# Contracting 64 rows in half the array: the third part of the first layer in the seven smallest experts

## The chip, the cores and the metric

The kernel runs on one core of one Trainium2 chip. The metric is device microseconds of one execution, the median of three. Engines are named as the profile names them: PE is TensorE's matmuls, PEld its weight loads, DVE is VectorE, ACT is ScalarE, POOL is GpSimd, SP is SyncE.

## The reference

A gated recurrent attention over 4 batches, 8 heads, 768 steps and head size 40 gives 3072 tokens of 320 features; a two-level mixture of 16 experts follows. Each token picks a group and, in it, an expert, and only that expert's two layers are applied to it:

```python
for g in range(G):                       # 4 groups
    mask_g = g_idx == g                  # g_idx = argmax(x @ w_group)
    xg = x[mask_g]
    e_logits = xg @ w_expert[g]
    e_idx = np.argmax(e_logits, axis=1)
    ...
    for e in range(Eg):                  # 4 experts of a group
        mask_e = e_idx == e
        h = np.maximum(xg[mask_e] @ w1[g, e], 0.0)      # 320 -> 1024
        ye = h @ w2[g, e]                               # 1024 -> 320
        out[tok_idx] = combined[:, None] * ye
```

## The kernel before

The attention comes first, in units of 128 steps of one batch. Its rows `x` go to DRAM as 384 columns, the 320 features and then the last 64 of them a second time (`store`). Tokens are routed while the attention runs. Then the experts follow one after another, ordered by how many tokens they have, the largest first. Expert `r` has room for `CAPS[r]` tokens; the last seven, `FULL` (`r` = 9 to 15), have room for 160, 144, 144, 144, 128, 128 and 96. This number is `W` (`W1` in `expert`).

For each expert its token rows are gathered (`load_x`), turned on PE (`turn_tasks`, L314) into `xhl`, features on partitions and tokens along the free dimension, and two layers are computed. The 320 features are three parts of the contraction, `k` = 0, 1, 2, of 128, 128 and 64 rows. The first-layer weights are laid out by the host as three blocks of 128 rows; the third holds rows 256 to 319 twice, in partitions 0 to 63 and again in 64 to 127.

In a `FULL` expert both layers' operands are kept so that float32 products come out exactly enough: the first layer multiplies plain float32 tiles, and each such matmul is two instructions on PE (48 in the profile for 24 in the code). The first layer's 1024 outputs are 8 groups of 128 (`NF`), two of them side by side in one PSUM bank `psh`, from the pool `ps_h` with three buffers. Each group is opened by its `k` = 0 product. The third product contracts all 128 partitions, with the lower half of `xhl[:, 2]` set to zero by POOL (L691); ACT copies the rest of `xhl` in two pieces per block of tokens (L692, L693).

`relu` empties a bank. Where `W` is 160 or 144 it is three steps: DVE writes the last 32 or 16 tokens to `hf` (L720), ACT writes the rounded part of `hh` (L722), and DVE the remainder of `hh` (L725). Where `W` is 128 or 96, `hf` falls away. After each bank one quarter of the next expert's second-layer weights is split into two parts, by ACT (L651) and DVE (L653); this is `between`. After the first layer PE turns the next expert's tokens (L314) and then runs the second layer (L796 to L798 for a block of tokens over 64, three products for each of the 8 groups; L788 for the 16 or 32 tokens that are left over, in four column strips). Its sums `po` are scaled into `y` (L808, or L810 to L813 for the left-over tokens, on ACT and DVE) and scattered to the output by POOL (L592).

```python
W1, rest = W, key[0] > 1 and mo == 32          # rest: the last 32 or 16 tokens apart
...
if rest:
    nc.vector.tensor_scalar(hf[:, f:f + per, :], src[:, :, W:], 0.0, None, op0=ALU.max)
act = nc.scalar.activation(hr, src, AF.Relu)
```

The code up to unit 22 of the attention is issued in the order written; after that the framework's scheduler orders each engine's queue from its own estimate of when operands are ready, with the order of the code as priority. Each engine works its queue in order. The bank named `av` belongs to the pool `ps_1` and serves the attention and the third token block of wide experts.

Of the kernel before, what the change touches and what calls it, by code (L numbers as in the profile page):

```python
# [7 lines left out]
F32 = mybir.dt.float32  # L8
F32R = mybir.dt.float32r
BF16 = mybir.dt.bfloat16  # L10
# [8 lines left out]
P = 128  # L19
# [6 lines left out]
F = 1024  # L26
NF = F // P
# [26 lines left out]
def bc(ap, shape):  # L54
    return ap.broadcast_to(list(shape))
# [3 lines left out]
def lstm_moe(ctx: ExitStack, tc: tile.TileContext, gates, qkT, nat, og, wcat, w1, w2, cst, out):  # L59
    nc = tc.nc  # L60
    enter = ctx.enter_context
    mm = nc.tensor.matmul
# [8 lines left out]
    const = enter(tc.tile_pool(name="const", bufs=1))  # L71
# [6 lines left out]
    ones_b = const.tile([P, P], BF16, name="ones_b")  # L78
# [10 lines left out]
    ohsum = [const.tile([P, NE], BF16, name=f"ohsum{i}") for i in range(2)]  # L89
    sep = const.tile([1, 1], F32, name="sep")  # L90
    neg_b = const.tile([P, P], BF16, name="neg_b")
    wk2 = enter(tc.tile_pool(name="wk2", bufs=2))
    ps_1 = enter(tc.tile_pool(name="ps_1", bufs=1, space=PSUM))
    post = enter(tc.tile_pool(name="post", bufs=2, reuse_waits="tile"))
# [545 lines left out]
    pools = {}  # L640
# [36 lines left out]
    def turn_tasks(key, W, xg, banks=None):  # L677
        t = {}

        def one(i, m):  # L680
            if i == 0:
                pool = pools["xhl"][len(xhls) % len(pools["xhl"])]
                sh, dt = ([P, 3, W], F32) if key[0] in FULL else ([P, 3, 2, W], F32R)
                t["x"] = xhls[key] = pool.tile(sh, dt, name="xhl", bufs=1)
            xhl, g = t["x"], xg[i]
            pool, tag = (banks or ((ps_1, "tp"), (ps_1, "lg"), (ps_1, "av")))[i]
            tp = pool.tile([P, 3, P], F32, name="tpm", tag=tag)
            turned(tp, g)
            if key[0] in FULL:
                if i == 0:  # L690
                    nc.gpsimd.memset(xhl[64:P, 2, :], 0.0)  # L691
                nc.scalar.copy(xhl[:, 0:2, i * P:i * P + m], tp[:, 0:2, 0:m])  # L692
                nc.scalar.copy(xhl[0:64, 2, i * P:i * P + m], tp[0:64, 2, 0:m])  # L693
                return
            xh = xhl[:, :, 0, i * P:i * P + m]
            nc.scalar.copy(xh, tp[:, :, 0:m])  # L696
            nc.vector.tensor_tensor(xhl[:, :, 1, i * P:i * P + m], tp[:, :, 0:m], xh.bitcast(F32), op=ALU.subtract)

        return [lambda i=i, m=m: one(i, m) for i, m in enumerate(blocks(W))]

    def expert(key, W, ws, xg, idx, between=(), then=None, last=None):
        xhl = xhls[key]
# [14 lines left out]
        def relu(f, per, src):  # L717
            hr = hh[:, f:f + per, 0:W]
            if rest:
                nc.vector.tensor_scalar(hf[:, f:f + per, :], src[:, :, W:], 0.0, None, op0=ALU.max)  # L720
                src = src[:, :, 0:W]
            act = nc.scalar.activation(hr, src, AF.Relu)  # L722
            for dst, t in ((slice(wl, wl + nf), slice(0, nf)), (slice(nf + mo, wl), slice(nf, W))):
                if t.start < t.stop:
                    nc.vector.scalar_tensor_tensor(hh[:, f:f + per, dst], src[:, :, t], 0.0, hr.bitcast(F32)[:, :, t],  # L725
                                                   op0=ALU.max, op1=ALU.subtract)
            return act

        if key[0] in FULL:
            w1s = w1st[key[0]]  # L730
            for f in range(0, NF, 2):
                ps = pools["ps_h"].tile([P, 512], F32, name="psh")
                for g in range(2):
                    for k in range(3):
                        s = slice(k * F + (f + g) * P, k * F + (f + g + 1) * P)
                        ins = mm(ps[:, g * W1:(g + 1) * W1], w1s[:, s], xhl[:, k, :], start=(k == 0), stop=(k == 2))  # L736
                relu(f, 2, ps[:, 0:2 * W1].rearrange("p (q w) -> p q w", q=2))
                do(between, 1)
        elif key in NARROW:
            xw, xh = [xhl[:, k].rearrange("p a w -> p (a w)") for k in range(3)], [xhl[:, k, 0, :] for k in range(2)]  # L740
            for f in range(0, NF, 2):
                hs = pools["hp"].tile([P, 2, W], F32, name="hs", bufs=2)
                for g in range(2):
                    ps = pools["ps_h"].tile([P, 512], F32, name="psh")
                    s0 = slice((f + g) * P, (f + g + 1) * P)
                    s1 = slice(F + (f + g) * P, F + (f + g + 1) * P)
                    mm(ps[:, 0:2 * W], w1h[:, s0], xw[0], start=True, stop=False)
                    mm(ps[:, 0:W], w1l[:, s0], xh[0], start=False, stop=False)
                    mm(ps[:, 0:W], w1l[:, s1], xh[1], start=False, stop=False)
                    mm(ps[:, 0:2 * W], w1h[:, s1], xw[1], start=False, stop=False)  # L750
                    ins = mm(ps[:, 0:2 * W], wsk[:, s0], xw[2], start=False, stop=True)
                    nc.scalar.copy(hs[:, g, :], ps[:, W:2 * W])
                    nc.vector.tensor_tensor(hs[:, g, :], hs[:, g, :], ps[:, 0:W], op=ALU.add)
                act = relu(f, 2, hs)
                if key[0] == 0:
                    do(between, 1)
        else:
            per = 2 if W1 <= 256 else 1
            for f in range(0, NF, per):
                ps = pools["ps_h"].tile([P, 512], F32, name="psh")  # L760
                for g in range(per):
                    s0 = slice((f + g) * P, (f + g + 1) * P)
                    s1 = slice(F + (f + g) * P, F + (f + g + 1) * P)
                    xh, xl = [xhl[:, k, 0, :] for k in range(3)], [xhl[:, k, 1, :] for k in range(3)]
                    todo = [(w1h, s0, xh[0]), (w1h, s0, xl[0]), (w1h, s1, xh[1]), (w1h, s1, xl[1]), (wsk, s0, xh[2]),
                            (wsk, s0, xl[2]), (w1l, s0, xh[0]), (w1l, s1, xh[1])]
                    for n, (w, s, x) in enumerate(todo):
                        ins = mm(ps[:, g * W1:(g + 1) * W1], w[:, s], x, start=(n == 0), stop=(n == len(todo) - 1))  # L768
                relu(f, per, ps[:, 0:per * W1].rearrange("p (q w) -> p q w", q=per))
                if per == 2 or f % 2:  # L770
                    do(between, 1)
# [206 lines left out]
    with tc.manual_schedule():  # L978
        nc.sync.dma_start(G[:, 0], gates[0:BH])
        nc.scalar.dma_start(cs, cst)  # L980
        nc.scalar.dma_start(G[:, 1], gates[BH:2 * BH])
        nc.scalar.dma_start(G4, gates[2 * BH:])
        nc.vector.memset(ones_b, 1.0)
        nc.vector.memset(sep, 0.0)
        nc.scalar.activation(sep, sep, AF.Exp)
        busy(11)
        nc.vector.memset(ones4, 1.0)
        nc.vector.memset(Dl[:, 0, 0:1], 0.0)
        nc.vector.memset(Apc[96:P], 0.0)
        for t in qkp[0:2]:  # L990
            nc.gpsimd.memset(t[0:Z], 0.0)
        load_qk(0)
        loads(0)
        load_o(0)
        load_qk(1)
        loads(1)
        loads(2)
        nc.scalar.copy(sel_b, cs[:, C_SEL:C_SEL + B * H])
        nc.scalar.copy(lt_b, cs[:, C_LT:C_LT + P])
        nc.scalar.activation(neg_b, ident, AF.Copy, scale=NEG)  # L1000
        sums.append(gate_sums(0))
        sum_on(9)
        for t in kws:
            nc.gpsimd.memset(t, 0.0)
        for t in qkp[2:]:
            nc.gpsimd.memset(t[0:Z], 0.0)
        nc.gpsimd.memset(Cflat, 0.0)
        nc.gpsimd.tensor_copy(id_b, ident)
        decay(0, 0)
        decay(0, 1, pool=ps_1, tag="lg")  # L1010
        scores(0)
        keyw(0)
        masked(0, 0)
        masked(0, 1)
        carried(0)
        carried2(0)
        sums.append(gate_sums(1))
        decay(1, 0)
        values(0)
        gate_o(0)  # L1020
        decay(1, 1, pool=ps_1, tag="lg")
        state(0)
        sum_on(3)
        keyw(1)
        nc.gpsimd.iota(tokid, pattern=[[P, NBLK]], base=0, channel_multiplier=1)
        nc.gpsimd.tensor_copy(keyb, cs[:, C_15E:C_15E + NE])
        nc.gpsimd.tensor_copy(base_b, cs[:, C_BASE:C_BASE + NE])
        nc.gpsimd.memset(ohsum[0], 0.0)
        loads(3)
        nc.sync.dma_start(wc, wcat)  # L1030
        unit(1, first=True)
        sum_on(9)
        sums.append(later_sums())
        sum_on(1)
        for u in range(2, 10):
            unit(u)
            do(due if u in (2, 6) else [])
            sum_on({2: 2, 3: 3, 4: 2, 5: 9}.get(u, 0))
# [211 lines left out]
```

## Time and profile before

| | |
|---|---|
| median of three runs | 399.18 us |
| the three runs | 398.45, 399.18, 400.91 us |
| the profiled execution | 398.51 us, of which the span from first to last instruction is 396.9 us |
| mean granted clock of TensorE in it | 0.981 |
| busy in the span | PE 379.4 us (96%), DVE 267.0 (67%), ACT 212.8 (54%), POOL 175.0 (44%) |

The span leaves 1.6 us of the execution's time outside. Busy time of PE is modelled for pipelined matmuls: several are in flight at a time, so the pace of a group is read from starts, and not from the mean duration of one instruction. A row of the timeline gives start, time from the first start to the last end, engine, line, what is written from what, and the count; in brackets is the idle time before it.

### The profile page before, as it was taken

What the parts mean: (1) busy time and instruction counts of PE and PEld (TensorE: products, weight loads), DVE (VectorE), ACT (ScalarE), POOL (GpSimd) and SP (SyncE); (2) the same over time, 40 slices, a digit from 0 to 9 for tenths busy, and PEclk for the clock granted to TensorE, in tenths of its full rate; (3) what the DMA queues carried; (4) which work ended last, traced back from release to release, by engine and by line L of the source; (5) the groups of instructions that cost most, each with busy time, mean ns of one, the idle gap of its engine ahead of it and who ended that gap; (6) DMA issues with size and microseconds to landing.
All of it is one profiled execution on the core that took longest, in us unless ns stands there. A gap on an engine that the chain in (4) does not pass through costs nothing.

```text
span 396.9 us, 9817 instructions
## 1 busy us (share of the span) xinstructions
PE 379.4 (96%) x3673; PEld 349.4 (88%) x3673; DVE 267.0 (67%) x702; ACT 212.8 (54%) x544; POOL 175.0 (44%) x231
## 2 busy tenths in 40 slices
PE   8989999999999977999999999999999999999994
PEld 4778998889899866799999998999999998888994
DVE  4777777998888944874957768756745666555520
ACT  5765565666656501625655566656655645445520
POOL 7445576476675544356432206352142315232310
PEclk9999999999999988699999999999999999999999
DMA  7976559999898217029951369996664537887700
GB/s 235 274 225 207 156 80 308 269 322 228 190 304 152 88 23 215 3 61 335 411 207 53 112 250 362 414 310 232 248 226 151 185 110 253 318 307 269 282 18 10
DMA packets 28340, 83.38 MB, mean 210 GB/s; under 512 B 11463, under 2 KB 15550, under 8 KB 24708
## 3 DMA queue, kind: packets, MB, share of 16 engines
q1 hardware_dynamic: 22724, 64.74, 52.1%
q0 software_dynamic: 5232, 17.65, 13.2%
q8 instruction: 29, 0.48, 0.5%
q10 hardware_dynamic: 336, 0.36, 0.3%
q14 instruction: 19, 0.16, 0.2%
HBM read 72.97 MB, written 9.99 MB: 209 GB/s over the span
## 4 chain that ended last, share of the span: by engine, by line
PE 71%; issue 8%; DVE 8%; DMA 7%; POOL 2%; ACT 1%; POOLq 1%; DVEq 0%; SPq 0%; ACTq 0%
PE psh L768 11%; PE av L284 10%; PE psh L736 6%; PE po L796 5%; PE po L798 5%; PE po L797 5%; PE sp L212 5%; PE it L237 4%; DMA itab<-tokid,slot 3%; PE aw L185 3%; PE it L256 2%; PE tpm L314 2%; PE po L788 2%; DMA w1s<-in_w_dram 2%; PE busy L127 2%
## 5 line engine op out<-in xcount | busy, mean ns | idle before, releaser
L195 ACT ACTIVATE ab<-aw,bcol 128x128 f32<-128x128 f32 x192 | 54.6, 371 | 38.0 <-PE aw L185 36.1
L592 POOL DMA_INDIRECT out_dram<-y,ix x32 | 36.1, 1128 | 70.3 <-ACT y L808 61.8
L588 POOL DMA_INDIRECT xg<-x_d,ix x32 | 35.8, 1119 | 64.7 <-DMA ix<-itab 40.0
L796 PE MATMUL po<-w2h,hh 128*128 128x320 f32 (+3 forms) x200 | 63.1, 316 | 0.8 <-ACT hh L722 0.8
L798 PE MATMUL po<-w2h,hh 128*128 128x320 f32 (+3 forms) x200 | 61.9, 310 | 0.0
L797 PE MATMUL po<-w2l,hh 128*128 128x320 f32 (+3 forms) x200 | 61.7, 309 | 0.0
L768 PE MATMUL psh<-xhl,w1hl 128*128 128x256 f32 (+5 forms) x336 | 53.9, 290 | 0.9 <-ACT xhl L696 0.4
L653 DVE TENSOR_TENSOR w2l<-w2s,w2h 128x640 fp32r<-128x640 f32 x52 | 41.0, 818 | 17.2 <-ACT w2h L651 17.1
L284 PE MATMUL av<-nt,pt 128*128 128x128 f32 x384 | 49.1, 283 | 2.3 <-DVE pt L217 2.3
L284 PEld LDWEIGHTS av<-nt,pt 128*128 128x128 f32 x384 | 46.3, 197 | 3.2 <-DVE pt L217 3.2
L768 PEld LDWEIGHTS psh<-xhl,w1hl 128*128 128x128 f32 x336 | 46.7, 193 | 1.9 <-PE psh L768 0.8
L722 ACT ACTIVATE hh<-psh 128x256 fp32r<-128x256 f32 (+5 forms) x68 | 29.1, 431 | 35.3 <-DVE hf L720 17.6
L736 PEld LDWEIGHTS psh<-xhl,w1s 128*128 128x128 f32 x336 | 40.9, 191 | 2.9 <-ACT y L808 2.1
L736 PE MATMUL psh<-xhl,w1s 128*128 128x144 f32 (+3 forms) x336 | 42.5, 285 | 0.2
L725 DVE SCALAR_TENSOR_TENSOR hh<-psh,hh 128x256 fp32r<-128x256 f32 (+4 forms) x76 | 32.7, 445 | 14.7 <-ACT hh L722 13.7
L217 DVE TENSOR_TENSOR pt<-sp,ab 128x512 f32<-128x512 f32 x48 | 30.9, 686 | 14.6 <-PE sp L212 11.3
L808 ACT ACTIVATE y<-po,xg 128x320 f32<-128x320 f32 (+3 forms) x25 | 13.2, 529 | 49.5 <-PE po L798 48.6
L796 PEld LDWEIGHTS po<-w2h,hh 128*128 128x128 f32 (+3 forms) x200 | 36.5, 182 | 2.2 <-ACT hh L722 1.1
L798 PEld LDWEIGHTS po<-w2h,hh 128*128 128x128 f32 (+3 forms) x200 | 36.4, 182 | 0.2
L797 PEld LDWEIGHTS po<-w2l,hh 128*128 128x128 f32 (+3 forms) x200 | 36.4, 182 | 0.0
L651 ACT CAST w2h<-w2s 128x640 fp32r<-128x640 f32 x52 | 35.1, 725 | 0.9 <-DMA w2s<-in_w_dram 0.9
L496 POOL DMA_INDIRECT itab<-tokid,slot x24 | 27.1, 1129 | 16.6 <-DVE slot L430 6.6
(217 smaller groups left out, 733.0 us busy)
## 6 DMA issues: line engine op xcount, KB each, us to landing
w1s<-in_w_dram SPq DMA_DIRECT2D x12, 1536.0 KB, 8.1
w2s<-in_w_dram SPq DMA_DIRECT2D x9, 1280.0 KB, 9.4
nt<-in_nat_dram SPq DMA_DIRECT2D x24, 324.0 KB, 6.4
qk<-in_qkT_dram SPq DMA_DIRECT2D x24, 320.0 KB, 7.5
x_d<-x SPq DMA_DIRECT2D x24, 192.0 KB, 5.9
sig<-in_og_dram SPq DMA_DIRECT2D x6, 640.0 KB, 8.2
w1hl<-in_w_dram SPq DMA_DIRECT2D x3, 1280.0 KB, 10.1
w1s<-in_w_dram SPq DMA_DIRECT2D x4, 768.0 KB, 7.2
```

The source lines that it names most:

```text
L195: rt["exp"] = nc.scalar.activation(st_[u]["ab"][:, r, j, :], aw[:, j, :], AF.Exp, bias=bcol[:, c, i:i + 1])
L284: ins = mm(av[:, i:i + P], t["pm"][r][:, pr, :], nt[:, o:o + P], start=True, stop=True)
L588: return nc.gpsimd.indirect_dma_start(out=o, out_offset=None, in_=src, in_offset=bass.IndirectOffsetOnAxis(ap=idx, axis=0))
L592: return nc.gpsimd.indirect_dma_start(out=out, out_offset=bass.IndirectOffsetOnAxis(ap=idx, axis=0), in_=y, in_offset=None, bounds_check=N ...
L651: nc.scalar.copy(a, src[:, s])
L653: lows.append(lambda: nc.vector.tensor_tensor(o[rows], src[rows, s], a[rows].bitcast(F32), op=ALU.subtract))
L725: nc.vector.scalar_tensor_tensor(hh[:, f:f + per, dst], src[:, :, t], 0.0, hr.bitcast(F32)[:, :, t], op0=ALU.max, op1=ALU.subtract)
L736: ins = mm(ps[:, g * W1:(g + 1) * W1], w1s[:, s], xhl[:, k, :], start=(k == 0), stop=(k == 2))
L768: ins = mm(ps[:, g * W1:(g + 1) * W1], w[:, s], x, start=(n == 0), stop=(n == len(todo) - 1))
L796: mm(po[0:m], hh[:, f, t], w2h[:, s], start=st0, stop=False)
L797: mm(po[0:m], hh[:, f, t], w2l[:, s], start=False, stop=False)
L798: ins = mm(po[0:m], hh[:, f, tl], w2h[:, s], start=False, stop=sp0)
```

## The change

For the seven `FULL` experts the first layer's order changes. All four PSUM banks of the layer are taken at once, three `psh` and the bank `av`. Each is opened by one bfloat16 matmul of zeros (weights `zero_b`, 64 rows) over its whole width of `2 * W1` columns. Then come all eight third parts, each as a contraction of 64 rows: the banks 0 and 2 use partitions 0 to 63 of weights and tokens, the banks 1 and 3 use partitions 64 to 127, in turn. Then come the first and second parts of all eight groups, bank after bank, each bank followed by its `relu` and one task of `between`. The lower half of `xhl[:, 2]` holds the second copy of the 64 features and is no longer zeroed, and one ACT copy per block takes all three parts. `zero_b` is a new constant of 128x128 bfloat16, set by POOL near the start.

```diff
+    zero_b = const.tile([P, P], BF16, name="zero_b")
...
             if key[0] in FULL:
-                if i == 0:
-                    nc.gpsimd.memset(xhl[64:P, 2, :], 0.0)
-                nc.scalar.copy(xhl[:, 0:2, i * P:i * P + m], tp[:, 0:2, 0:m])
-                nc.scalar.copy(xhl[0:64, 2, i * P:i * P + m], tp[0:64, 2, 0:m])
+                nc.scalar.copy(xhl[:, :, i * P:i * P + m], tp[:, :, 0:m])
                 return
...
         if key[0] in FULL:
             w1s = w1st[key[0]]
-            for f in range(0, NF, 2):
-                ps = pools["ps_h"].tile([P, 512], F32, name="psh")
+            banks = [pools["ps_h"].tile([P, 512], F32, name="psh") for _ in range(3)]
+            banks.append(ps_1.tile([P, 512], F32, name="psh", tag="av"))
+
+            def part(i, g, k, rs, **kw):
+                s = k * F + (2 * i + g) * P
+                return mm(banks[i][:, g * W1:(g + 1) * W1], w1s[rs, s:s + P], xhl[rs, k, :], **kw)
+
+            halves = slice(0, 64), slice(64, P)
+            for i in range(4):
+                rs = halves[i % 2]
+                mm(banks[i][:, 0:2 * W1], zero_b[rs], bc(ones_b[rs, 0:W1 // 2].unsqueeze(1), (64, 4, W1 // 2)),
+                   start=True, stop=False)
+            for i in (0, 2):
                 for g in range(2):
-                    for k in range(3):
-                        s = slice(k * F + (f + g) * P, k * F + (f + g + 1) * P)
-                        ins = mm(ps[:, g * W1:(g + 1) * W1], w1s[:, s], xhl[:, k, :], start=(k == 0), stop=(k == 2))
-                relu(f, 2, ps[:, 0:2 * W1].rearrange("p (q w) -> p q w", q=2))
+                    for r in range(2):
+                        part(i + r, g, 2, halves[r], start=False, stop=False)
+            for i in range(4):
+                for g in range(2):
+                    for k in range(2):
+                        ins = part(i, g, k, slice(0, P), start=False, stop=(g == 1 and k == 1))
+                relu(2 * i, 2, banks[i][:, 0:2 * W1].rearrange("p (q w) -> p q w", q=2))
                 do(between, 1)
...
         for t in kws:
             nc.gpsimd.memset(t, 0.0)
+        nc.gpsimd.memset(zero_b, 0.0)
         for t in qkp[2:]:
             nc.gpsimd.memset(t[0:Z], 0.0)
```

## Rows read from the trace of the kernel before

**Rows 1.** Page, part 1: busy us, share of the span, instructions.

```profile
PE 379.4 (96%) x3673; PEld 349.4 (88%) x3673; DVE 267.0 (67%) x702; ACT 212.8 (54%) x544; POOL 175.0 (44%) x231
```

**Rows 2.** Busy time by stretch: PE, PEld, DVE, ACT, POOL, then PEclk, DMA share, GB/s.

```profile
340.90:347.70 6.80, 6.73 (x57) 6.54 (x55) 6.26 (x15) 3.48 (x8) 2.51 (x2) 1.00 0.78 322
347.70:352.60 4.90, 4.90 (x43) 3.88 (x41) 0.59 (x2) 1.90 (x8) 1.37 (x3) 1.00 0.93 330
```

**Rows 3.** Timeline of PE: the first layer of experts 9, 11, 13, 15, and its end.

```profile
317.10 6.68 PE L736 MATMUL psh<-xhl,w1s 128*128 128x160 f32 x48
323.62 0.82 PE L314 MATMUL tpm<-cs,xg 128*128 128x128 f32 x6
...
340.85 6.46 PE L736 MATMUL psh<-xhl,w1s 128*128 128x144 f32 x48
347.14 0.82 PE L314 MATMUL tpm<-cs,xg 128*128 128x128 f32 x6
...
364.04 5.62 PE L736 MATMUL psh<-xhl,w1s 128*128 128x128 f32 x48
369.50 0.49 PE L314 MATMUL tpm<-cs,xg 128*128 128x128 f32 x3
...
382.55 5.50 PE L736 MATMUL psh<-xhl,w1s 128*128 128x96 f32 x48
387.83 0.37 PE L796 MATMUL po<-w2h,hh 128*96 128x320 f32 x1
```

**Rows 4.** Timeline of PE, narrow windows in expert 10's first layer.

```profile
329.10 0.39 PE L736 MATMUL psh<-xhl,w1s 128*128 128x144 f32 x1
...
329.10 0.64 PE L736 MATMUL psh<-xhl,w1s 128*128 128x144 f32 x3
...
329.10 4.68 PE L736 MATMUL psh<-xhl,w1s 128*128 128x144 f32 x36
...
333.83 0.61 PE L736 MATMUL psh<-xhl,w1s 128*128 128x144 f32 x3
```

**Rows 5.** Timeline of PE, narrow windows around the attention's scores and carried products.

```profile
101.74 0.22 PE L185 MATMUL aw<-Apc,sel_b 128*128 128x128 bf16 x1
...
101.89 0.49 PE L212 MATMUL sp<-qk 64*128 64x128 f32 x4
...
101.89 1.16 PE L212 MATMUL sp<-qk 64*128 64x128 f32 x16
...
103.74 0.28 PE L237 MATMUL it<-Cflat,qk 64*128 64x128 f32 x2
103.95 0.23 PE L185 MATMUL aw<-Apc,sel_b 128*128 128x128 bf16 x1
```

**Rows 6.** Timeline of PE near the start: bfloat16 products of 512 columns.

```profile
6.29 0.38 PE L182 MATMUL aw<-neg_b,lt_b 128*128 128x512 bf16 x1
6.50 0.38 PE L185 MATMUL aw<-Apc,sel_b 128*128 128x128 bf16 x4
```

**Rows 7.** Groups of DVE from 280 us on: count, busy us, mean ns, idle before.

```profile
L653 DVE TENSOR_TENSOR w2l<-w2s,w2h 128x640 fp32r<-128x640 f32 x20 | 15.6, 817 | 8.5 <-ACT w2h L651 8.4
L725 DVE SCALAR_TENSOR_TENSOR hh<-psh,hh 128x256 fp32r<-128x256 f32 x24 | 10.0, 418 | 2.0 <-ACT hh L722 1.5
L812 DVE TENSOR_TENSOR y<-y,po 16x320 f32<-16x320 f32 x9 | 4.4, 483 | 0.3
L720 DVE TENSOR_SCALAR hf<-psh 128x32 f32<-128x32 f32 x12 | 2.2, 180 | 1.1 <-PE psh L736 1.1
```

**Rows 8.** Waits from 314 us on: us in total, times, longest us.

```profile
ACT hh L722 <- DVE hf L720: 12.8, 15, 2.2
```

**Rows 9.** Timeline of POOL, and of PE, near the start.

```profile
9.60 0.28 POOL L1008 CAST id_b<-cs 128x128 bf16<-128x128 f32 x1
9.85 0.93 POOL L224 TENSOR_TENSOR kw<-nt,ab 128x320 f32<-128x320 f32 x1
...
11.69 0.67 PE L256 MATMUL it<-nt,kw 128*64 128x41 f32 x16
```

## The prediction, made before the run

> **What bounds the kernel now.** I read the page's busy shares first: PE is at 96% and no other engine is over 67% [rows 1]. The share alone doesn't say that the changed stretch is bound by PE, so the second view is the busy time by stretch, for the first and the second layer of one of the seven experts [rows 2]: PE is busy 6.73 of 6.80 us and 4.90 of 4.90 us, at full granted clock (1.00, the 2.4 GHz level). DVE is the one to watch beside it: 6.26 us of the first layer's stretch, but only 0.59 of the second's. In the third view, the timeline of PE, one expert's first layer starts right behind the other's second layer, and the turning products behind that [rows 3]. So what is taken from PE in this stretch comes off the end of the kernel, unless a wait takes its place. The DMA share is 0.78 and 0.93 in the two stretches [rows 2]; the period is 11.75 us (329.10 to 340.85 [rows 4, 3]) and would be about 8% shorter, so the mean share would go from 0.84 to about 0.91. The weights of an expert are asked for almost two periods ahead, so I count no wait for them.
>
> **The pace of the first layer.** All 48 instructions of an expert go through PE in turn. At `W` = 160 it is 6.52 us / 48 = 136 ns each (317.10 to 323.62 [rows 3]). At 144, from the third to the 36th, (4.68 - 0.64) / 33 = 122 ns [rows 4]. At 128, (5.46 - 0.10) / 48 = 112 ns, with 0.10 us for a slow first instruction, explained below. At 96, 5.28 / 48 = 110 ns [rows 3]: hardly less than at 128, so there something other than the token columns sets the pace. A third of these 48, 16 per expert, is the third part.
>
> **What halves cost.** The trace has float32 products in halves: the attention's scores, 16 instructions in turn on partitions 0 to 63 and 64 to 103, 128 columns each. From the fourth to the sixteenth they take (1.16 - 0.49) / 6 = 112 ns for two [rows 5], against 112 ns for one over all rows at the same width. So two halves run in the time of one, weight loads included. The 16 become 8 pairs at the pace above, and 8 paces are saved: 1.09 us at 160, 0.98 at 144 (three experts), 0.89 at 128 (two), 0.88 at 96. Together 6.70 us.
>
> The Trainium skill, "TensorE: Matmul & The Clock Gate", section "LDWEIGHTS (loading the stationary operand)", speaks against this: a load's time goes by its columns, so 32 rows cost what 128 cost. If the loads of two halves came one after the other, the 6.70 us would be nothing. The scores' row contradicts that for halves in turn (two loads of 128 columns within 112 ns), and the same page, section "Part 3: Packing small matmuls — row/col tiling", says that a load overlaps with matmuls in other rows. It stays as a rival with a small chance.
>
> **A wait that goes.** In experts 10, 11 and 12 PE stands still before the fourth bank: the 36th instruction ends at 333.78, the third of the fourth bank at 334.44, 0.66 us later, where three paces are 0.37 [rows 4]. That is 0.29 us. `ps_h` has three buffers, and the fourth bank waits for the first to be emptied, which DVE does late: ACT's `hh` waits 12.8 us in all for DVE's `hf` [rows 8]. With four banks at once this wait has no place any more: 3 x 0.29 = 0.87 us saved. The other experts show no such gap: 5.46 us at 128 and 6.52 at 160 are 48 even paces.
>
> **The zeros.** Four matmuls of `2 * W1` columns in bfloat16. A product of 512 such columns takes 0.21 us over all rows (6.29 to 6.50 [rows 6]), 0.41 ns a column, with a moving operand that repeats as the zeros' does. No row has bfloat16 in halves. At best two run together, as in the scores: two pairs are 0.26, 0.24, 0.21 and 0.16 us at the four widths, 1.55 us in all seven. At worst they run one by one, 3.10 us. I take 1.55, since the scores are the nearest row and differ only in type; the 1.55 between stays in the range.
>
> **Changes between whole rows and halves.** Entering halves, the scores start 0.15 us after the last `aw` (101.74 to 101.89 [rows 5]), where `aw` products follow each other at (0.38 - 0.22) / 3 = 0.05 us [rows 6]: 0.10 more. Leaving, `aw` starts 0.21 us after the last pair (103.74 to 103.95), 0.10 over a pair's 0.11. The first float32 product after such a change takes 0.39 us (329.10 [rows 4]); two more add only 0.25, so an ordinary one is about 0.29: another 0.10. Leaving thus costs 0.20, seven times: 1.40. Experts 9, 14 and 15 come from whole rows and pay 0.10 on entering: 0.30. Experts 10 to 13 come from the column strips of L788 and pay a change already, 0.10 of it for a slow first float32, which zeros in bfloat16 may not need: minus 0.40. Whether the first float32 pair behind the zeros is slow by 0 or 0.10 no row tells: I take 0.05, 0.35 in all, and keep plus or minus 0.35. Sum 1.65 us.
>
> **Edits with cover.** The memset of `zero_b` stands in POOL's queue ahead of two memsets, a copy and `keyw` of unit 0; a copy of the same tile shape takes 0.28 us [rows 9]. `keyw` ends at 10.78 and PE reads it at 11.69, so 0.9 us of PE's earlier work hides it; without that cover it would cost its 0.28 once. The zeroing of `xhl` goes from POOL, one of ACT's two copies per block goes, and ACT is busy only half of the stretch: nothing on the path, and gathers queued behind the zeroing come sooner.
>
> **What is late next.** The first relu now comes after the zeros, all third parts and one bank: 0.24 + 1.03 + 0.20 + 8 x 0.122 + 0.29 in flight = 2.74 us at `W` = 144, where it was 0.10 + 12 x 0.122 + 0.29 = 1.86. The second layer comes sooner: 5.4 us for the first layer and 0.66 for six turning products (0.11 each, (0.82 - 0.49) / 3 [rows 3]), so at 6.0. By then DVE must have the first `hh`, the last about 2.7 us later (about three quarters of 4.9 us [rows 2] are the large block's, 0.9 us a bank). DVE has 6.26 + 0.59 = 6.85 us of work in a period, 4 x (0.42 + 0.18) = 2.4 of it for the relus [rows 2, 7], the rest, 4.45, splitting weights and left-over tokens of the expert before. If all the rest goes first, the first `hh` is there at 0.1 + 4.45 + 0.18 + 0.4 for ACT + 0.42 = 5.6, and the last at about 7.4, before 8.7. The cover is thin at its start (0.4 us) and wider at its end. I count nothing.
>
> **The sum.** 6.70 + 0.87 - 1.55 - 1.65 = 4.4 us less. Against the profiled execution: 398.51 - 4.4 = 394.1 us. That execution is 0.67 under the median of the three, 399.18; on that scale it is 394.8 us, which I predict. By width: about 0.5 us at 160, 0.95 in each at 144, 0.6 in the first at 128, 0.4 in the others.
>
> **Rivals.**
> - *Zeros one by one.* For: no row shows bfloat16 in halves. Against: the scores. 1.55 us less gain, 396.3.
> - *The second layer waits for DVE, in part.* DVE is 92% busy in the first layer's stretch, and the order in its queue is the scheduler's. For each of experts 10 to 13 a few tenths, 1.2 us in all: 396.0. For: the 0.4 us of cover. Against: DVE is nearly idle in the second layer, so a delay isn't handed on.
> - *Slower: DVE's queue holds the first relu in the wrong place.* Place: the first L796 behind L314 in experts 10 to 13. If `hf` of the first bank keeps its early place in DVE's queue, DVE stands 0.9 us for a bank that is not full, with weight splitting behind it, and if the first `hh` comes last, it is there at 6.85 + 0.9 = 7.7 us and not at 6.0. That is 1.7 us in each of four, 6.8 against a gain of 4.4: 401.6. It turns slower from 1.1 us in each. Against: the scheduler follows readiness, and in the trace the relus stand between the splits, not behind them.
> - *The halves don't pay.* If loads don't overlap, the 6.70 of the sum goes, and 6.70 - 4.4 = 2.3 us are lost: 401.5. Against: the scores' 112 ns.
>
> **How the numbers follow.** The forecast gets 0.62 (its own range, from the slow first pairs and the spread of medians, 394.0 to 395.8), zeros one by one 0.12, the partial wait 0.15, slower by DVE 0.04, halves that don't pay 0.03, and 0.04 for a gain of over 5 us, from a better order on DVE and ACT. The range takes the first three and their overlap: 393.4 to 397.8. About 1% is what a measurement of this kernel tells from no change, as its three runs spread by 0.6%: the line is at 395.2 us. Two thirds of the forecast's chance and the better case lie below, little of the others: faster 0.48, within 1% 0.48, slower 0.04 (only the two bad rivals at their worst).
>
> **What would show it.** Right: in the changed timeline of PE, third parts in pairs at one pace per pair, zeros starting in twos, 32 instructions at the old pace, no gap before the fourth bank; first layers of 6.0, 5.4, 4.9 and 4.9 us; L796 starting behind L314 without a wait. Wrong: zeros in single file; idle time of PE at L796 with DVE's `hh` as releaser; a weight load of L736 waiting for DMA as periods shorten; or the queues of other stages coming out in another order.

## The result, and the profile after

The changed kernel takes 395.18 us, median of 9 runs, against 399.27 us for the kernel before, median of 9 measured beside it: ratio 0.9892, 95% interval 0.9860 to 0.9925. By the ratio that is 4.3 us or 1.1% faster, and the interval reaches from 3.0 to 5.6 us; 4.4 us and 394.8 us had been predicted. The ratios leave out executions in a slower state, two of the changed kernel's nine, so that 4.3 us isn't the difference of the two medians. The changed kernel's profiled execution took 395.18 us, 393.5 of it the span.

All experiments are also compared by one length of the trace that the rest of the kernel doesn't touch: from the start of the first product of expert 9's first layer to the start of the last product of expert 15's second layer. I call it the stretch. The kernel before: the first product is at 317.10 [rows 3], the last in this row.

```profile
391.26 0.31 PE L798 MATMUL po<-w2h,hh 128*96 128x320 f32 x1
```

The stretch before is 391.26 - 317.10 = 74.16 us. The timeline of PE of the changed kernel, with the zeros (L739) and the other products of the first layer (L734) of the four experts of [rows 3], what follows them, and the last product:

```profile
317.84 0.45 PE L739 MATMUL psh<-ones_b,zero_b 64*128 64x320 bf16 x4
318.12 5.79 PE L734 MATMUL psh<-xhl,w1s 64*128 64x160 f32 x48
323.75 0.82 PE L315 MATMUL tpm<-cs,xg 128*128 128x128 f32 x6
...
340.06 0.42 PE L739 MATMUL psh<-ones_b,zero_b 64*128 64x288 bf16 x4
340.32 5.26 PE L734 MATMUL psh<-xhl,w1s 64*128 64x144 f32 x48
345.42 0.82 PE L315 MATMUL tpm<-cs,xg 128*128 128x128 f32 x6
...
361.38 0.39 PE L739 MATMUL psh<-ones_b,zero_b 64*128 64x256 bf16 x4
361.61 4.83 PE L734 MATMUL psh<-xhl,w1s 64*128 64x128 f32 x48
366.27 0.49 PE L315 MATMUL tpm<-cs,xg 128*128 128x128 f32 x3
...
379.30 0.34 PE L739 MATMUL psh<-ones_b,zero_b 64*128 64x192 bf16 x4
...
387.49 0.31 PE L810 MATMUL po<-w2h,hh 128*96 128x320 f32 x1
```

The stretch is 387.49 - 317.84 = 69.65 us, 4.51 less. The first layers are 5.91 us at `W` = 160 (317.84 to 323.75), 5.36 at 144, 4.89 at 128 and 4.76 at 96 (379.30 to 384.06), where the prediction had 6.0, 5.4, 4.9 and 4.9. In a second profiled execution the stretch is 69.35 (385.15 - 315.80); there expert 14 has no pause ahead of its turning products, in the first it has 0.21 us. A candidate is the gather of expert 15's tokens (L589 on POOL), which these products turn. They start 8.94 us after the gather's start in the execution with the pause (366.38 to 375.32), 9.06 us after it in the other (364.01 to 373.07), and 10.37 us after it before the change (368.33 to 378.70). In a run without zeros that pauses in the same place the profile has the gather landing 8.7 us after its issue. So the shorter periods leave this gather hardly any cover. The profile doesn't name it as the cause, and no run tests it.

```profile
315.80 0.45 PE L739 MATMUL psh<-ones_b,zero_b 64*128 64x320 bf16 x4
...
385.15 0.30 PE L810 MATMUL po<-w2h,hh 128*96 128x320 f32 x1
```

A narrow window of PE in expert 11 of the changed kernel, beside the row of all four above, shows how the zeros run:

```profile
340.06 0.30 PE L739 MATMUL psh<-ones_b,zero_b 64*128 64x288 bf16 x2
```

Two are over after 0.30 us and all four after 0.42: 0.12 a pair, the time of one by the price of [rows 6]. They run in twos. The page's busy shares, and the busy time by stretch for expert 11 (columns as in rows 2):

```profile
PE 375.2 (95%) x3701; PEld 344.6 (88%) x3701; DVE 267.2 (68%) x702; ACT 211.8 (54%) x533; POOL 173.3 (44%) x225
```

```profile
340.06:346.00 5.94, 5.94 (x63) 5.77 (x59) 5.60 (x12) 2.94 (x7) 1.49 (x2) 1.00 0.94 370
346.00:350.88 4.88, 4.88 (x43) 3.85 (x40) 1.25 (x5) 2.32 (x7) 1.39 (x3) 1.00 0.87 316
```

PE has no idle time in either; the gap ahead of the fourth bank is gone. DVE has the same 6.85 us of work (5.60 + 1.25), but more of it lies in the second layer's stretch than in [rows 2]. The period is 10.83 us (340.06 to the next zeros at 350.89), the DMA share 0.94 and 0.87, and no wait for a weight transfer shows in the stretch. DVE's queue in expert 11:

```profile
340.14 1.56 DVE L654 TENSOR_TENSOR w2l<-w1hl,w2h 128x640 fp32r<-128x640 f32 x2 [2.83 <-ACT w2h L652]
...
343.39 0.81 DVE L654 TENSOR_TENSOR w2l<-w1hl,w2h 128x640 fp32r<-128x640 f32 x1
344.22 0.49 DVE L824 TENSOR_TENSOR y<-y,po 16x320 f32<-16x320 f32 x1
344.74 0.19 DVE L718 TENSOR_SCALAR hf<-psh 128x32 f32<-128x32 f32 x1
...
345.14 0.17 DVE L718 TENSOR_SCALAR hf<-psh 128x32 f32<-128x32 f32 x1
345.45 0.76 DVE L723 SCALAR_TENSOR_TENSOR hh<-psh,hh 128x256 fp32r<-128x256 f32 x2
```

The scheduler put all four weight splits and three of the four steps for the left-over tokens ahead of the first `hf`. The first of the two `hh` steps in the last row is over at about 345.87, 5.8 us after the first product of zeros. The second layer's first product is at 345.99, and the remainder is first read by its third product, about 0.38 us later (0.23 and 0.15 between the first three starts). So PE doesn't wait, with 0.5 us to spare here. Expert 12 turns only three blocks, and its second layer starts 5.6 us after its first product of zeros (350.89 to 356.49). There the first `hh` step is over at about 356.69, 5.8 us after the zeros again, and the third product starts at 356.86: about 0.2 us to spare.

```profile
356.27 0.76 DVE L723 SCALAR_TENSOR_TENSOR hh<-psh,hh 128x256 fp32r<-128x256 f32 x2
...
356.86 0.31 PE L810 MATMUL po<-w2h,hh 128*128 128x320 f32 x1
```

### The profile page after: what moved, and what is told of

It reads as the page before. It is cut to its first block, busy times and chain, and to the rows that moved or that the text cites. A ratio compares the mean times of both kernels' runs of the same rounds, so it can differ in the third digit from the quotient of the medians.

```text
span 393.5 us, 9840 instructions
## 1 busy us (share of the span) xinstructions
PE 375.2 (95%) x3701; PEld 344.6 (88%) x3701; DVE 267.2 (68%) x702; ACT 211.8 (54%) x533; POOL 173.3 (44%) x225
## 4 chain that ended last, share of the span: by engine, by line
PE 75%; issue 7%; DMA 6%; DVE 6%; ACT 2%; POOL 2%; POOLq 1%; SPq 0%; DVEq 0%; ACTq 0%
PE psh L780 13%; PE av L285 10%; PE sp L213 6%; PE psh L734 5%; PE po L808 5%; PE po L810 5%; PE po L809 5%; PE it L238 5%; PE aw L186 3%; PE it L257 3%; PE tpm L315 2%; PE tp L315 2%; DMA ix<-itab 2%; DMA w1s<-in_w_dram 2%; DMA w2s<-in_w_dram 2%
## 5 line engine op out<-in xcount | busy, mean ns | idle before, releaser
L593 POOL DMA_INDIRECT out_dram<-y,ix x32 | 37.3, 1165 | 78.6 <-ACT y L820 62.7
L589 POOL DMA_INDIRECT xg<-x_d,ix x32 | 34.3, 1073 | 63.9 <-DMA ix<-itab 43.5
L285 PE MATMUL av<-nt,pt 128*128 128x128 f32 x384 | 47.6, 277 | 1.6 <-DVE pt L218 1.6
L780 PEld LDWEIGHTS psh<-xhl,w1hl 128*128 128x128 f32 x336 | 47.5, 195 | 1.8 <-PE psh L780 0.8
L285 PEld LDWEIGHTS av<-nt,pt 128*128 128x128 f32 x384 | 44.7, 192 | 2.5 <-DVE pt L218 2.5
L734 PE MATMUL psh<-xhl,w1s 128*128 128x144 f32 (+7 forms) x336 | 36.0, 284 | 0.0
L734 PEld LDWEIGHTS psh<-xhl,w1s 128*128 128x128 f32 (+1 forms) x336 | 34.4, 190 | 1.1 <-issue 0.2
```

The costliest lines, as they stand in the source:

```text
L285: ins = mm(av[:, i:i + P], t["pm"][r][:, pr, :], nt[:, o:o + P], start=True, stop=True)
L589: return nc.gpsimd.indirect_dma_start(out=o, out_offset=None, in_=src, in_offset=bass.IndirectOffsetOnAxis(ap=idx, axis=0))
L593: return nc.gpsimd.indirect_dma_start(out=out, out_offset=bass.IndirectOffsetOnAxis(ap=idx, axis=0), in_=y, in_offset=None, bounds_check=N ...
L734: return mm(banks[i][:, g * W1:(g + 1) * W1], w1s[rs, s:s + P], xhl[rs, k, :], **kw)
```

## The experiments

In this table "whole" is the ratio of the whole time to the kernel before measured beside it, with its 95% interval (one for each time that the kernel was measured), and "against changed" is the stretch less the 69.35 us of the changed kernel's undisturbed execution. The stretch without zeros is that of two executions without a pause in expert 14; the third had the pause, and 68.64 us.

| kernel | whole | stretch, us | against changed | expected |
|---|---|---|---|---|
| changed, first run | 0.9892 (0.9860 to 0.9925) | 69.65 | | |
| changed, again | 0.9866 (0.9830 to 0.9902) | 69.35 | | |
| four banks alone | 0.9995 (0.9977 to 1.0013), 0.9987 (0.9954 to 1.0019) | 73.20 | | 73.29 |
| all in one half | 1.0109 (1.0084 to 1.0133) | 77.68 | +8.33 | +8.2 |
| two rounds of two banks | 0.9963 (0.9942 to 0.9985) | 71.50 | +2.15 | +2.1 |
| no zeros | 0.9845 (0.9823 to 0.9867), 0.9861 (0.9821 to 0.9902), 0.9885 (0.9851 to 0.9918) | 68.48 | -0.87 | -1.0 |
| one split on DVE done twice | 0.9907 (0.9876 to 0.9938) | 70.19 | +0.84 | +1.7 |
| two splits done twice | 0.9898 (0.9864 to 0.9932) | 70.28 | +0.93 | +5 |
| six splits ahead of the relus | 1.0110 (1.0061 to 1.0158) | 76.67 | +7.32 | +6.5 |

**The changed kernel once more.** 

> The changed kernel once more, beside the others on one chip. From the first run: a ratio of 0.989 to the kernel before, and in the trace 69.65 us from the first product of expert 9's first layer to the last product of expert 15's second, where the kernel before has 74.16.

The ratio is 0.9866 where 0.989 was expected, within its interval, and the stretch 69.35 us without the pause in expert 14. The two ratios differ by 0.3%, about 1 us, which is as fine as whole times can be compared here; the stretch, where nothing pauses, repeats to a few hundredths: 73.20 twice with four banks, 68.48 twice without zeros.

**Four banks alone.** 

> The kernel before with one part of the change alone: four banks taken at once (three psh and av), products over all rows in the old order. Theory of the sum: the gap ahead of the fourth bank in experts 10 to 12 goes, 0.29 us each, 0.87 us in all, nothing else: 398.4 us. Rival (the gain of the change is mostly the freed wait and what follows from it on DVE and ACT, and not the halves): 3 us or more less than before, under 396.3 us. Rival (the wait only moves to the start of the second layer): same as before, 399.3 us.

```diff
+            banks = [pools["ps_h"].tile([P, 512], F32, name="psh") for _ in range(3)]
+            banks.append(ps_1.tile([P, 512], F32, name="psh", tag="av"))
             for f in range(0, NF, 2):
-                ps = pools["ps_h"].tile([P, 512], F32, name="psh")
+                ps = banks[f // 2]
```

> The four banks alone once more. The first run's trace had 0.96 us less from expert 9's first product to expert 15's last, but its ratio was 0.9995 (0.9977 to 1.0013). Theory of the sum: the 0.96 us is in the whole time too, a ratio of 0.9976. Rival (what the seven experts gain is lost elsewhere): 1.000 again.

The timeline of PE of the second run, expert 11's first layer, the start of the stretch and its end:

```profile
317.02 6.68 PE L738 MATMUL psh<-xhl,w1s 128*128 128x160 f32 x48
...
340.48 6.15 PE L738 MATMUL psh<-xhl,w1s 128*128 128x144 f32 x48
...
390.22 0.30 PE L800 MATMUL po<-w2h,hh 128*96 128x320 f32 x1
```

Expert 11's 48 instructions take 6.15 us where they took 6.46 [rows 3]: 0.31 less, in each of three experts. The stretch is 73.20, 0.96 less than before, in both executions, and the second layer follows without a wait. So the freed wait is real and is a fifth of the gain; the halves, less what the zeros and the changes of mode cost, are the rest. In the whole time the two ratios give 0.2 and 0.5 us less. The second interval holds the expected 0.9976, the first just doesn't (0.9977): the whole times are too coarse to confirm 0.96 us, and don't show a loss elsewhere either.

**All in one half.** 

> The changed kernel with all zeros and third parts in partitions 0 to 63, so that no two halves stand beside each other; the sums are the same, since both halves hold the same 64 rows. Theory of the sum: a half alone costs as much as all rows, and only running two at a time pays. The 16 instructions of the third part take 16 paces and not 8 (6.70 us in seven experts), the four zeros run one by one (1.55 us): 8.2 us slower than the changed kernel, 403.4 us. Rival (64 rows are cheaper by themselves, for the weight load or the product): the third part stays near 8 paces, under 398 us.

```diff
-            halves = slice(0, 64), slice(64, P)
+            halves = slice(0, 64), slice(0, 64)
```

Its timeline of PE, expert 11, and the ends of the stretch:

```profile
314.73 0.71 PE L739 MATMUL psh<-ones_b,zero_b 64*128 64x320 bf16 x4
...
339.53 0.66 PE L739 MATMUL psh<-ones_b,zero_b 64*128 64x288 bf16 x4
340.03 6.24 PE L734 MATMUL psh<-xhl,w1s 64*128 64x144 f32 x48
...
392.41 0.30 PE L810 MATMUL po<-w2h,hh 128*96 128x320 f32 x1
```

The 48 instructions take 6.24 us and not 5.26: 0.98 us more, which is 8 paces of 0.122. The zeros take 0.66 and not 0.42, one by one. A product of 64 rows by itself costs as much as one of 128, for both types; what the change gains by the halves it gains by two at a time alone. The kernel is 1.1% slower than the one before. The weight loads of the first layers in the changed kernel, over all rows and in halves (count, busy us, mean ns):

```profile
L734 PEld LDWEIGHTS psh<-xhl,w1s 128*128 128x128 f32 x224 | 27.2, 191 | 0.9 <-issue 0.2
...
L734 PEld LDWEIGHTS psh<-xhl,w1s 64*128 64x128 f32 x112 | 7.2, 187 | 0.1
```

A load of 64 rows takes 187 ns and one of 128 rows 191. The rule of the Trainium skill that a weight load's time goes by its columns ("TensorE: Matmul & The Clock Gate", section "LDWEIGHTS (loading the stationary operand)") agrees with these rows. It doesn't speak against the change, because loads for two halves overlap: 112 of 187 ns lie within 7.2 us, 2.9 at a time, where those over all rows are 1.6 at a time.

**Two rounds of two banks.** 

> The changed kernel with the first layer in two rounds of two banks: zeros and third parts of banks 0 and 1, their first and second parts, then the same for banks 2 and 3. One more way into halves and out of them per expert. Theory of the sum: 0.10 us to enter and 0.20 us to leave, seven times, 2.1 us slower than the changed kernel, 397.3 us; in the timeline 0.30 us per expert. Rival (the changes of mode are hidden by the weight loads): no difference, 395.2 us. Rival (DVE is the hidden limit): the first relu comes 0.7 us sooner, which gives back part of it.

```diff
-            for i in range(4):
-                rs = halves[i % 2]
+            for j in (0, 2):
+                for i in (j, j + 1):
+                    rs = halves[i % 2]
...
-            for i in (0, 2):
-                for g in range(2):
-                    for r in range(2):
+                for i in (j,):
+                    for g in range(2):
+                        for r in range(2):
...
-            for i in range(4):
-                for g in range(2):
-                    for k in range(2):
+                for i in (j, j + 1):
+                    for g in range(2):
+                        for k in range(2):
```

Its timeline of PE in expert 11, and the ends of the stretch:

```profile
315.10 0.31 PE L740 MATMUL psh<-ones_b,zero_b 64*128 64x320 bf16 x2
...
337.95 0.30 PE L740 MATMUL psh<-ones_b,zero_b 64*128 64x288 bf16 x2
338.08 2.81 PE L734 MATMUL psh<-xhl,w1s 64*128 64x144 f32 x24
340.82 0.30 PE L740 MATMUL psh<-ones_b,zero_b 64*128 64x288 bf16 x2
340.96 2.81 PE L734 MATMUL psh<-xhl,w1s 64*128 64x144 f32 x24
...
386.60 0.31 PE L811 MATMUL po<-w2h,hh 128*96 128x320 f32 x1
```

The stretch is 2.15 us longer for seven more ways in and out, 0.31 each, where 0.10 + 0.20 had been read from [rows 4] and [rows 5]. The price of a change between whole rows and halves holds, and nothing of it came back from a first relu that comes sooner.

**No zeros.** 

> Leaves out the four products of zeros; the first third part in each bank opens the bank instead. Theory of the sum (PE's stream sets the end, every term is on the path): the zeros' own time goes, 0.26 us at 144 columns and 1.7 us in all seven experts, but the first pair that enters the halves is now float32 and slow by 0.10 us, 0.7 us in all. The first layers become 0.16 us shorter each and the kernel about 1.0 us faster than the changed one: about 394.2 us. Rival (the zeros hide the change into halves, or the banks' opening has to wait anyway): no difference, 395.2 us. Rival (after the zeros go, DVE's first remainder of hh is late, because its cover in the changed kernel is 0.15 us): first layers 0.16 us shorter, but the second layer starts as late as before in experts 10 to 13, and only 0.5 us is gained.

```diff
-            for i in range(4):
-                rs = halves[i % 2]
-                mm(banks[i][:, 0:2 * W1], zero_b[rs], bc(ones_b[rs, 0:W1 // 2].unsqueeze(1), (64, 4, W1 // 2)),
-                   start=True, stop=False)
...
-                        part(i + r, g, 2, halves[r], start=False, stop=False)
+                        part(i + r, g, 2, halves[r], start=(g == 0), stop=False)
```

> The kernel without the products of zeros once more, on the same chip as the changed kernel. Theory of the sum: 1.0 us less than the changed kernel, 0.25% of the time, as its stretch showed (68.64 against 69.65 us). Rival: the 1.8 us less that its ratio showed (0.9845 against 0.9892) is real, and something outside the seven experts gained too; then the ratio is below 0.986 again.

> Without the products of zeros, a third time, for its ratio. From the stretch of the seven experts 0.87 us less than the changed kernel: by the three ratios of that one so far (0.9892 and 0.9866) about 0.986.

From the third run's timeline of PE:

```profile
316.00 5.90 PE L734 MATMUL psh<-xhl,w1s 64*128 64x160 f32 x48
...
337.89 5.37 PE L734 MATMUL psh<-xhl,w1s 64*128 64x144 f32 x48
...
384.48 0.31 PE L806 MATMUL po<-w2h,hh 128*96 128x320 f32 x1
```

The 48 instructions take 5.37 us where the changed kernel's 48 take 5.26, so 0.11 of the zeros' 0.26 comes back as the slow first pair; 0.15 us per expert is gained, 0.87 in the stretch. The zeros do cost their time, less what they take from the way into halves. The whole times follow only in part: 0.9845, 0.9861 and 0.9885 stand beside 0.9892 and 0.9866 for the changed kernel. Against the kernel before this version is faster beyond doubt; against the changed kernel the stretch shows a gain of 0.87 us, and whole times can't tell. That something outside the seven experts gained too, 1.8 us in all, isn't borne out: the second and third ratio aren't below 0.986 again.

**One split on DVE done twice.** 

> The changed kernel, with one of the four DVE steps that split the next expert's second-layer weights done twice, for experts 9 to 15: 0.82 us more work on DVE per expert, the same numbers. It tests the cover that the prediction called thin. In the changed kernel the first remainder of hh is done 5.8 us after the first product of zeros in expert 11, where PE needs it at 6.3; 5.8 against 6.0 in expert 12; 5.1 against 5.5 in expert 13. Theory (DVE does the splits first, then the relus, and PE waits for the first remainder): later by 0.82 less the cover, 0.3 us in experts 10 and 11, 0.6 in 12, 0.4 in 13, 1.7 us in all, 396.9 us. Rival (DVE's idle second-layer time takes it up): no difference, 395.2 us.

```diff
+            if r in FULL and h == "w2h" and s.start == 0:
+                lows.append(lambda: nc.vector.tensor_tensor(o[rows], src[rows, s], a[rows].bitcast(F32), op=ALU.subtract))
```

Half the expected loss: from one expert's zeros to the next's it is 0.16 us in experts 10 and 11, 0.51 in 12 and nothing in 13. DVE's and PE's timelines in expert 12, whose first layer starts at 354.41:

```profile
359.50 0.17 DVE L720 TENSOR_SCALAR hf<-psh 128x32 f32<-128x32 f32 x1
359.60 0.80 DVE L654 TENSOR_TENSOR w2l<-w2s,w2h 128x640 fp32r<-128x640 f32 x1
360.33 0.74 DVE L725 SCALAR_TENSOR_TENSOR hh<-psh,hh 128x256 fp32r<-128x256 f32 x2
...
360.25 0.31 PE L811 MATMUL po<-w2l,hh 128*128 128x320 f32 x1
360.79 0.41 PE L812 MATMUL po<-w2h,hh 128*128 128x320 f32 x1 [0.24 <-DVE hh L725]
```

The scheduler put the fifth split behind the second `hf` and ahead of the first `hh`, partly in the time in which DVE had waited for ACT, so the remainder came 0.5 us later and not 0.8. PE's third product (L812), the first that reads the remainder, starts 0.54 us behind the second instead of 0.15. The wait is where the prediction's rival had it, and the cover is as thin as that said.

**Two splits done twice.** 

> As the last, with two of the four steps done twice: 1.64 us more on DVE per expert. Theory: 1.1 us of wait in experts 10 and 11, 1.5 in 12, 1.2 in 13, 5 us in all, which eats the whole gain of the change: 400 us, about as the kernel before. Rival (the scheduler puts the relus ahead of the splits once they are ready, so that PE doesn't wait): under 397 us.

```diff
+            if r in FULL and h == "w2h" and s.start in (0, NF * DM // 4):
+                lows.append(lambda: nc.vector.tensor_tensor(o[rows], src[rows, s], a[rows].bitcast(F32), op=ALU.subtract))
```

Here the theory failed and the rival held: 0.93 us instead of 5. DVE's timeline in expert 11:

```profile
349.28 0.74 DVE L725 SCALAR_TENSOR_TENSOR hh<-psh,hh 128x256 fp32r<-128x256 f32 x2
...
350.04 0.80 DVE L654 TENSOR_TENSOR w2l<-w1hl,w2h 128x640 fp32r<-128x640 f32 x1
```

The sixth split went behind the first two `hh` steps, where DVE's slack in the second layer takes it. DVE's lateness is thus no sum of work; it is what the queue's order puts ahead of the first remainder, and the scheduler keeps that short.

**Six splits ahead of the relus.** 

> The changed kernel with two of the four weight splits on DVE done twice, as in the last experiment, and now all six queued on DVE ahead of the first relu of each of the seven experts. It builds the prediction's slower rival on purpose. Theory (a first remainder of hh that is late holds PE at the second layer, with its whole lateness): in experts 10 to 13 six splits of 0.81 us, three steps of 0.48 and one of 0.36 for the left-over tokens come first, so the first remainder is done about 7.8 us after the first product in experts 10 to 12 and 7.2 in expert 13, where PE needs it at 6.3, 6.3, 6.0 and 5.5: 1.5 + 1.5 + 1.8 + 1.7 = 6.5 us, none in 14 and 15. About 2 us slower than the kernel before, 401.5 us. Rival (PE's wait costs less, as other work of PE fills it, or later experts give it back): 397 us or less.

```diff
-                relu(2 * i, 2, banks[i][:, 0:2 * W1].rearrange("p (q w) -> p q w", q=2))
-                do(between, 1)
+                if i == 0:
+                    do(between)
+                with ExitStack() as st:
+                    if i == 0:
+                        st.enter_context(tc.issue_after(rt["low"].ins))
+                    relu(2 * i, 2, banks[i][:, 0:2 * W1].rearrange("p (q w) -> p q w", q=2))
```

Here `rt["low"]` is the last split on DVE, and two splits are done twice as in the last kernel. DVE's and PE's timelines at the end of expert 11's first layer, which starts at 341.75:

```profile
347.36 0.80 DVE L654 TENSOR_TENSOR w2l<-w1hl,w2h 128x640 fp32r<-128x640 f32 x1
348.19 0.39 DVE L720 TENSOR_SCALAR hf<-psh 128x32 f32<-128x32 f32 x3
...
348.89 1.09 DVE L725 SCALAR_TENSOR_TENSOR hh<-psh,hh 128x256 fp32r<-128x256 f32 x3 [0.32 <-ACT hh L722]
...
347.10 0.82 PE L315 MATMUL tpm<-cs,xg 128*128 128x128 f32 x6
348.92 0.41 PE L814 MATMUL po<-w2h,hh 128*128 128x320 f32 x1 [1.00 <-ACT hh L722]
```

With that order forced, DVE's lateness reaches PE, which stands idle for 1.00 us by this row, until ACT has the rounded part of `hh` that itself waited for `hf`. The stretch is 7.32 us longer, and the kernel 1.1% slower than before. From one expert's zeros to the next's, experts 10 to 13 take 1.4, 1.4, 1.8 and 1.5 us more, close to the 6.5 expected in all; the rest is lost in experts 9 and 14, where none was expected. So the step of the slower rival by which a late first `hh` holds PE is shown, at about the price that was worked out for it (6.8 us). The lateness itself was made by other means here, 1.6 us of further work per expert and a forced order; that the order of DVE's queue alone could cost as much was not run, and the changed kernel doesn't have that order.

## Why the prediction was right

- **PE sets the end.** Every term taken from or added to PE's stream moved the stretch by its size: +8.33 for 8.2, +2.15 for 2.1, -0.87 for 1.0. The span ends 5.6 to 6.4 us after the stretch in every profiled execution, so what the stretch gains the kernel gains, to within some tenths.
- **Halves in pairs: 6.70 us.** Right. In expert 11 the pairs take 5.10 us (340.32 to 345.42) less 32 paces of 0.122 and 0.20 for leaving, 0.98 us, 8 paces. The run in one half shows that nothing but the pairing does it.
- **The fourth bank's wait: 0.87 us.** Right, 0.96 in the run with four banks alone.
- **The zeros: 1.55 us.** In twos, as taken. From the first of them to the first third part it is 0.28, 0.25, 0.26, 0.25, 0.23, 0.23 and 0.18 us, 1.68 in all, 0.13 more than taken. The rival "one by one" is out.
- **Changes of mode: 1.65 us.** Entering and leaving are as read: 0.31 for both in the run with two rounds. The 0.35 for a slow first float32 pair behind the zeros wasn't needed: the first layer at 144 columns is 0.26 + 0.98 + 0.20 + 32 x 0.1225 = 5.36 us without it, and 5.36 is what it takes. This and the zeros' 0.13 are the small errors in the sum. With measured terms it is 6.70 + 0.96 - 1.68 - 1.30 = 4.68 us, between the 4.51 and 4.81 of the two executions. The edits counted as nothing (the zeroing, the ACT copy, the memset) weren't run apart; together with reading errors they are the 0.13 us that the sum leaves over against 4.81.
- **By width.** The prediction's list, 0.5, three times 0.95, 0.6 and twice 0.4, adds up to 4.75 and not to 4.4; its own terms give 0.88 at 144. From one expert's first product to the next's, the undisturbed execution gains 0.60 at 160, 0.92 to 0.94 at 144, 0.48 and 0.37 at 128 and, to the end of the stretch, 0.57 at 96.
- **What is late next.** The queue came in the order taken as the worst that was still covered: splits first. The first remainder came at 5.8 us, not 5.6. The prediction compared that with the second layer's start at 6.0; PE needs it only 0.38 us later, so the cover was 0.5 us in experts 10 and 11 and 0.2 in 12. In expert 12 the prediction's own comparison would have failed: with three blocks to turn the second layer starts at 5.6, ahead of the first remainder. That PE doesn't wait there rests on the 0.38 us that the prediction hadn't counted, which is luck. The partial wait did not happen.
- **DMA.** With a share of 0.94 and 0.87 in the two stretches, no weight load became late. The gather of the next expert's tokens wasn't among the things that the prediction counted; with shorter periods it has hardly any cover left at expert 15, and the 0.21 us pause may be its price.
- **The number.** The sum was low by some tenths: 4.51 and 4.81 us in the stretch against 4.4. That the whole time shows 4.3 us, 0.1 from the forecast, is luck: the ratio's interval is 3.0 to 5.6 us, and the second measurement gives 5.3.

## What to carry to other kernels

In these runs a contraction of 64 rows gives time back only where two such products on different partitions stand next to each other in the stream; one half alone costs a full product. The two of a pair wrote to different banks in every run, so whether one bank would do isn't shown. Gather all such products of a stage into one block, since each way in and out costs about 0.3 us here, and count it against the pace saved (0.12 us a pair). When products move ahead of the step that empties the banks, check which engine's queue the first result has to pass before the next stage, and in which order the work stands in it: 1.6 us of further work in each of seven experts cost 0.9 us in all where the scheduler placed it, and some 7 us where it was queued ahead.

## What the runs showed of the hardware that had not been expected

The first product of expert 9 starts at 317.10 and 317.84 us in the first executions of the two kernels, at 315.80 in another of the changed one, and at 321.03 in the run with one split twice, although the code ahead of it is the same in the changed kernels but for the doubled split, which first comes before expert 9. Busy time by stretch, core 0, PEclk in the third column from the end, for the changed kernel in its first execution, then again, then with one split twice:

```profile
130.00:180.00 50.00, 44.14 (x374) 39.46 (x374) 34.19 (x127) 16.49 (x39) 23.85 (x33) 0.83 0.31 78
```

```profile
130.00:180.00 50.00, 43.82 (x394) 39.39 (x392) 34.52 (x130) 17.38 (x42) 25.75 (x34) 0.90 0.32 85
```

```profile
130.00:180.00 50.00, 42.80 (x373) 38.18 (x372) 33.95 (x127) 16.31 (x39) 22.57 (x32) 0.86 0.24 66
180.00:220.00 40.00, 37.77 (x266) 36.77 (x266) 25.09 (x59) 22.86 (x50) 17.59 (x18) 0.96 0.66 250
```

Between 130 and 180 us, where the attention ends and PE waits for the routing (44.14 us busy of 50 in the first of these), the granted clock's mean is 0.83, 0.90 and 0.86, and PE gets through 374, 394 and 373 products; in the third the mean is below 1.00 once more after 180 us. Elsewhere up to 310 us it was 1.00 in the changed kernel's two executions. So this is the place where the executions part, by several us, more than most of the terms above: a reason to compare single stretches. How much of it is the clock and how much the waiting isn't shown. The mean clock alone doesn't order the starts: the run with all in one half has 0.86 there as well and starts expert 9 at 314.73.
